# Where a fused attention and MLP block issues its first gate and up weights, and how its first token tiles are transposed

## The chip, the core and the metric

The kernel runs on one core of one Trainium2 chip. The metric is the device time of one execution in microseconds (us), the median of three runs. A core has five engines that run side by side, each taking its own instructions in order: TensorE (PE, matmuls, with its weight loads as PEld), VectorE (DVE), ScalarE (ACT), GpSimd (POOL) and SyncE (SP), which here issues nearly all transfers. TensorE writes its results to PSUM; VectorE and ScalarE carry them on to SBUF, the working memory.

## The reference

One block with a norm ahead of each half: linear attention with 32 heads, then a gated MLP, on 2048 tokens of width 1024. Shortened:

```python
def attention(x, wqkv, wo):                      # x is the normalised input
    q, k, v = split(x @ wqkv)                    # 32 heads of 32
    phi = lambda t: where(t > 0, t + 1, exp(t)) + 1e-6
    pq, pk = phi(q), phi(k)
    kv, z = pk.T @ v, sum(pk)                    # per head, over all tokens
    return (pq @ kv / (pq @ z + 1e-6)) @ wo

def mlp(x, W_gate, W_up, W_down):                # F = 3584
    return (relu(x @ W_gate) * (x @ W_up)) @ W_down

h  = x + attention(layernorm(x), wqkv, wo)
h2 = h + mlp(layernorm(h), W_gate, W_up, W_down)
```

## The kernel before

The large matmuls are done by a Strassen scheme: seven products in place of eight, for which VectorE forms sums of operand blocks (`t1` to `t4` of weights, `hs` of the normalised tokens), and ScalarE takes snapshots (`m`, `u`) of partial results in PSUM. A scheduler orders the instructions of each engine when the kernel is built; the code gives the dependencies and a rough order.

**The start.** The first tiles of 128 tokens are normalised and then transposed on TensorE (`PE_T` is 4), the later ones by a DMA transpose. Sixteen matmuls on zeros keep TensorE busy meanwhile.

```python
def ln_T(t):
    ...                                          # bn_stats, bn_aggr: VectorE
    nc.scalar.activation(out=lnv, ..., func=ACT.Ln, ...)
    nc.scalar.activation(out=rstd, ..., func=ACT.Exp, scale=-0.5)
    xn = bwork.tile([P, D], BF16, tag="hn", bufs=HB, name="xn")
    if t == atiles[0]:
        for k in range(2):                       # the very first tile: VectorE, in two halves
            ks = slice(k * NW, (k + 1) * NW)
            nc.vector.tensor_scalar(out=xn[:, ks], in0=x_sb[:, ks], ...)
        transpose_in(t, xn)
        return
    nc.vector.scalar_tensor_tensor(out=nmr, ...)
    nc.scalar.activation(out=xn[:], in_=x_sb[:], func=ACT.Identity, bias=nmr, scale=rstd)
    if t not in atiles[:PE_T]:
        nc.sync.dma_start_transpose(out=xT[s][i][:, :, r:r + P], in_=xn[:])
        return
    transpose_in(t, xn)

def transpose_in(t, xn):
    s, i, r = place(t)
    for k in range(2):
        pt = pspool.tile([P, KH, P], BF16, tag="D", bufs=1, name="tp")     # one PSUM bank
        for kc in range(KH):                                              # KH = 4
            nc.tensor.transpose(pt[:, kc, :], xn[:, ...], ident[:])
        (nc.scalar.copy if k else nc.vector.tensor_copy)(
            out=xT[s][i][:, k * KH:(k + 1) * KH, r:r + P], in_=pt[:])
```

`k_plain` then multiplies each of the first four tiles with `wk` (16 matmuls of 512 columns for a tile, 8 for each half of `wk`), and `v_plain` with `wv`. `wk` is loaded in two halves of 1 MB, the x tiles between them.

**The attention stage and the weights of the first gate and up quads.** For each tile of tokens there is a chain of steps, each some steps behind the one before it (`LAG`):

```python
def nd():       # numerator and denominator: TensorE; reciprocal by Ln and Exp: ScalarE;
    ...         # the product o_sb: VectorE (L518)
def oT():       # DMA transpose of o_sb, issued by SyncE (L525)
def x_in():     # load of the residual x, SyncE (L529)
def wo_h():     # attn: TensorE (L541); + x and row sums: VectorE (L543); h to DRAM: SyncE (L546);
    ...         # squares, rstd and hn: ScalarE (L553 to L557); hn has two buffers
def hn_T():     # DMA transpose of hn, SyncE (L560); the sums hs follow on VectorE (L117 to L120)
```

Into this stage come the first weights of gate and up: two groups, each of `wg` and `wu` in two halves of 512 KB, so eight loads.

```python
def hold(dst, src):
    nc.gpsimd.tensor_copy(out=dst, in_=src)      # one element

def load(after=None, w_sb=w_sb, v=v, h=h):
    if after is not None:
        hold(w_sb[0:1, 0, h, 0:1], after)
    (nc.sync if after is None else nc.gpsimd).dma_start(
        out=w_sb[:, :, h, :], in_=v[:, :, h, g * GP * P:(g + 1) * GP * P])
...
for step in range(QSTEPS):
    ...
    attn_step(step)
    if step:
        for _ in range(-(-len(early_loads) // (QSTEPS - step))):
            early_loads.pop(0)(held[step][0:1, 0:1])       # held[step] is o_sb of this step
```

The copy of one element of `o_sb` into the weight tile makes the load wait until that step's `o_sb` is written; it paces the loads. The load itself is issued by GpSimd. The later groups, with no pacing, are issued by SyncE.

Of the kernel before, what the change touches and what calls it, by code (L numbers as in the profile page):

```python
# [7 lines left out]
ACT = mybir.ActivationFunctionType  # L8
ALU = mybir.AluOpType
FP32 = mybir.dt.float32  # L10
BF16 = mybir.dt.bfloat16
# [20 lines left out]
def block_kernel(ctx: ExitStack, tc: tile.TileContext, x, wqkv, wo, wg, wu, wd, out, H: int):  # L32
    nc = tc.nc
    P = 128
    xf = x.flatten_outer_dims()
    of = out.flatten_outer_dims()
    S, D = xf.shape
# [6 lines left out]
    NW = 512  # L44
# [3 lines left out]
    KH = KC // 2  # L48
# [23 lines left out]
    GP = 2  # L72
# [67 lines left out]
    def hold(dst, src):  # L140

        nc.gpsimd.tensor_copy(out=dst, in_=src)
# [68 lines left out]
    pspool = psctx.enter_context(tc.tile_pool(name="ps", bufs=1, space=PSUM))  # L211
    with ExitStack() as actx:
# [11 lines left out]
        def load_x(t):  # L224
            x_sb = bwork.tile([P, D], BF16, tag=("x_res", "oT")[atiles.index(t) % 2], bufs=XB, name="x_sb")
            nc.sync.dma_start(out=x_sb[:], in_=xf[t * P:(t + 1) * P, :])
            x_tiles[t] = x_sb
# [4 lines left out]
        def place(t):  # L232
            i, r = divmod(t * P, HS)
            s, r = divmod(r, SW)
            return s, i, r
# [3 lines left out]
        atiles = [t for u in units for t in u]  # L239
# [9 lines left out]
        def ln_T(t):  # L249
            if t not in x_tiles:  # L250
                load_x(t)
            x_sb = x_tiles.pop(t)
            s, i, r = place(t)
            stats = asmall.tile([P, 2, nc.vector.BN_STATS_DIM], FP32, tag="stats", name="stats")
            for k in range(2):
                nc.vector.bn_stats(out=stats[:, k, :], in_=x_sb[:, k * NW:(k + 1) * NW])
            mv = asmall.tile([P, nc.vector.BN_AGGR_DIM], FP32, tag="mv", name="mv")
            nc.vector.bn_aggr(out=mv[:], in_=stats[:])
            sm = asmall.tile([P, 3], FP32, tag="sma", name="sma")
            lnv, rstd, nmr = (sm[:, k:k + 1] for k in range(3))  # L260
            nc.scalar.activation(out=lnv, in_=mv[:, 1:2], func=ACT.Ln, bias=LN_EPS, scale=1.0)
            nc.scalar.activation(out=rstd, in_=lnv, func=ACT.Exp, scale=-0.5)
# [4 lines that stand above are left out]
                    nc.vector.tensor_scalar(out=xn[:, ks], in0=x_sb[:, ks], scalar1=mv[:, 0:1], scalar2=rstd,  # L267
                                            op0=ALU.subtract, op1=ALU.mult)
                transpose_in(t, xn)
                return  # L270
            nc.vector.scalar_tensor_tensor(out=nmr, in0=mv[:, 0:1], scalar=-1.0, in1=rstd, op0=ALU.mult, op1=ALU.mult)
            nc.scalar.activation(out=xn[:], in_=x_sb[:], func=ACT.Identity, bias=nmr, scale=rstd)
            if t not in atiles[:PE_T]:
                nc.sync.dma_start_transpose(out=xT[s][i][:, :, r:r + P], in_=xn[:])
                return
            transpose_in(t, xn)

        def transpose_in(t, xn):
            s, i, r = place(t)
            for k in range(2):  # L280
                pt = pspool.tile([P, KH, P], BF16, tag="D", bufs=1, name="tp")
                for kc in range(KH):
                    nc.tensor.transpose(pt[:, kc, :], xn[:, (k * KH + kc) * P:(k * KH + kc + 1) * P], ident[:])
                (nc.scalar.copy if k else nc.vector.tensor_copy)(
                    out=xT[s][i][:, k * KH:(k + 1) * KH, r:r + P], in_=pt[:])

        rk, k_sums = right_ops(wk_sb, tk)
# [91 lines left out]
        with tc.high_priority():  # L379
            zero = asmall.tile([P, NW], BF16, tag="zero", bufs=1, name="zero")  # L380
            nc.vector.memset(zero[:], 0.0)
            spin = pspool.tile([P, NW], FP32, tag="A", bufs=2, name="spin")
            for n in range(SPIN):
                nc.tensor.matmul(spin[:], lhsT=zero[:, 0:P], rhs=zero[:], start=True, stop=True)
            ln_T(atiles[0])
        ln_T(atiles[1])
        todo = atiles[2:8]
        for t in units[0]:
            k_plain(t)
            ln_T(todo.pop(0))  # L390
# [86 lines left out]
    def load_group(g):  # L477

        tiles, loads = [], []
        for nm, v in (("wg", wg_v), ("wu", wu_v)):  # L480
            w_sb = wpools[g % 2].tile([P, KC, 2, GP * P], BF16, tag=nm, name=nm)
            for h in range(2):
                def load(after=None, w_sb=w_sb, v=v, h=h):
                    if after is not None:
                        hold(w_sb[0:1, 0, h, 0:1], after)
                    (nc.sync if after is None else nc.gpsimd).dma_start(out=w_sb[:, :, h, :], in_=v[:, :, h, g * GP * P:(g + 1) * GP * P])
                loads.append(load)
            tiles.append(w_sb)
        return tiles, loads
# [389 lines left out]
    prv, k = None, 0  # L879
    for r, (wt, f, fi, toks) in enumerate(runs):  # L880
        w = [ops() for _, ops in now]
        later = []
        for n, s in enumerate(toks):
            first = n == 0 and isinstance(wt, int) and fi == 0
# [50 lines left out]
            if k == nwin - 3:  # L935
                for x in range(2):
                    t = wpools[1].tile([P, KC * 2 * GP * P], BF16, tag=("wg", "wu")[x], name="wd")
# [16 lines left out]
    for n in range(2):  # L954
        t = fpool.tile([P, 4 * D], BF16, tag="wraw", bufs=2, name="xd")
# [242 lines left out]
    for n in range(1, len(OUTER)):  # L1198
# [73 lines left out]
        else:  # L1272
            pss = []
            for p in range(4):
# [15 lines left out]
                v = ps[:].rearrange("p (t d) -> p t d", t=2)  # L1290
# [53 lines left out]
```

## Time and profile before

| | |
|---|---|
| median of three runs | 754.87 us (754.65 to 755.37) |
| profiled execution, first to last instruction | 753.1 us |
| mean granted clock of TensorE | 0.989 of full |
| busy share: PE, DVE, ACT, POOL | 97%, 75%, 43%, 2% |
| moved by DMA | 132.04 MB, mean 175 GB/s |

The rows of instructions and waits in the profile name the line, the engine, the operation and what it wrote and read; times without a unit are microseconds from the start of the span, and a bracket at the end of a row gives how long the engine stood idle before it and what ended that. A busy TensorE is not one at full speed: the granted clock tells how fast it went. "SPq" is SyncE issuing a transfer; the time to landing is that from the issue until all data have arrived.

### The profile page before, as it was taken

What the parts mean: (1) busy time and instruction counts of PE and PEld (TensorE: products, weight loads), DVE (VectorE), ACT (ScalarE), POOL (GpSimd) and SP (SyncE); (2) the same over time, 40 slices, a digit from 0 to 9 for tenths busy, and PEclk for the clock granted to TensorE, in tenths of its full rate; (3) what the DMA queues carried; (4) which work ended last, traced back from release to release, by engine and by line L of the source; (5) the groups of instructions that cost most, each with busy time, mean ns of one, the idle gap of its engine ahead of it and who ended that gap; (6) DMA issues with size and microseconds to landing.
All of it is one profiled execution on the core that took longest, in us unless ns stands there. A gap on an engine that the chain in (4) does not pass through costs nothing.

```text
span 753.1 us, 10572 instructions
## 1 busy us (share of the span) xinstructions
PE 729.8 (97%) x3967; PEld 384.2 (51%) x4020; DVE 563.0 (75%) x991; ACT 322.0 (43%) x580; POOL 12.9 (2%) x52
## 2 busy tenths in 40 slices
PE   8999999998988999999999999999999999999997
PEld 3444555444443444444444444444444458888666
DVE  6997654774767677687787778877877559997797
ACT  4785653877567555344444344444434220000000
POOL 0000000021100000000000000000000000000000
PEclk9999999999898999999999999999999999999999
DMA  9765003089587445244936439466574299887922
GB/s 317 165 133 154 0 1 112 1 175 217 111 181 178 125 106 168 70 129 130 260 125 183 140 129 314 149 208 233 196 242 163 85 380 362 312 291 294 315 73 84
DMA packets 139412, 132.04 MB, mean 175 GB/s; under 512 B 50912, under 2 KB 119904, under 8 KB 139360
## 3 DMA queue, kind: packets, MB, share of 16 engines
q1 hardware_dynamic: 127072, 119.03, 52.1%
q10 hardware_dynamic: 11136, 8.13, 3.4%
q0 software_dynamic: 1152, 4.19, 2.3%
q8 instruction: 31, 0.51, 0.3%
q14 instruction: 21, 0.17, 0.1%
HBM read 79.95 MB, written 39.85 MB: 159 GB/s over the span
## 4 chain that ended last, share of the span: by engine, by line
PE 79%; DVE 8%; ACT 6%; DMA 5%; issue 2%; SPq 0%; DVEq 0%; ACTq 0%
PE accA L785 22%; PE accY L785 8%; PE accX L785 8%; PE accA L1117 8%; PE Aq L298 4%; PE attn L541 3%; PE accA L946 3%; PE accX L1117 3%; PE Aq L438 3%; PE accY L1117 2%; DMA hn<-hn 2%; PE Eq L298 2%; PE Aq L705 2%; PE accY L946 2%; PE accX L946 2%
## 5 line engine op out<-in xcount | busy, mean ns | idle before, releaser
L795 ACT ACTIVATE gu<-gu 128x512 bf16<-128x512 bf16 x72 | 45.4, 630 | 131.4 <-DVE gu L794 131.4
L790 ACT COPY snap<-accA 128x1024 f32<-128x1024 f32 x72 | 72.5, 1008 | 36.4 <-PE accA L785 36.2
L541 PE MATMUL attn<-wo_mem,oT 128*128 128x512 bf16 x249 | 61.6, 396 | 1.0 <-DVE o_sb L518 0.4
L785 PEld LDWEIGHTS <-tu 128*128 128x128 f16 x384 | 37.6, 98 | 45.3
L785 PEld LDWEIGHTS <-tg 128*128 128x128 f16 x384 | 37.6, 98 | 45.3
L794 DVE TENSOR_TENSOR gu<-accY,snap 128x1024 bf16<-128x1024 f32 x36 | 43.9, 1218 | 9.7 <-ACT snap L790 9.6
L154 ACT COPY u<-Aq 128x512 f32<-128x512 f32 x56 | 32.4, 582 | 39.9 <-PE Aq L298 19.6
L785 PE MATMUL accA<-hn,tu 128*128 128x512 f16 (+1 forms) x192 | 49.3, 379 | 0.0
L785 PE MATMUL accA<-hn,tg 128*128 128x512 f16 (+1 forms) x192 | 49.3, 379 | 0.0
L794 DVE TENSOR_TENSOR gu<-accX,snap 128x1024 bf16<-128x1024 f32 x36 | 43.9, 1218 | 6.5 <-PE accX L785 3.7
L1117 PEld LDWEIGHTS <-x 128*128 128x128 f16 (+1 forms) x448 | 43.8, 98 | 5.5
L785 PEld LDWEIGHTS <-wu 128*128 128x128 bf16 x288 | 28.2, 98 | 34.0
L785 PEld LDWEIGHTS <-wg 128*128 128x128 bf16 x288 | 28.2, 98 | 34.0
L541 PEld LDWEIGHTS <-oT 128*128 128x128 bf16 x256 | 25.7, 102 | 33.3 <-issue 7.1
L543 DVE SCALAR_TENSOR_TENSOR x_res<-attn,x_res 128x512 bf16<-128x512 f32 x32 | 21.8, 687 | 14.2 <-PE attn L541 14.2
L798 DVE TENSOR_TENSOR hq<-gu 128x512 bf16<-128x512 bf16 x48 | 20.3, 423 | 14.6 <-ACT gu L795 14.5
L298 PEld LDWEIGHTS <-xT 128*128 128x128 bf16 (+1 forms) x192 | 18.6, 98 | 24.2 <-issue 2.7
L1117 PEld LDWEIGHTS <-xs 128*128 128x128 f16 x280 | 27.4, 98 | 3.2
L946 PEld LDWEIGHTS <-x 128*128 128x128 bf16 (+1 forms) x168 | 16.4, 98 | 19.6
L1123 DVE TENSOR_TENSOR snap<-accA,u 128x1024 f32<-128x1024 f32 x16 | 19.5, 1219 | 8.3 <-PE accA L1117 8.1
L518 DVE TENSOR_TENSOR o_sb<-nd,rd 128x384 bf16<-128x384 f32 (+1 forms) x48 | 22.5, 505 | 3.9 <-ACT rd L517 3.8
L785 PE MATMUL accA<-hn,wu 128*128 128x512 bf16 x96 | 24.6, 379 | 0.0
(234 smaller groups left out, 1413.6 us busy)
## 6 DMA issues: line engine op xcount, KB each, us to landing
x<-x_dram SPq DMA_DIRECT2D x17, 896.0 KB, 8.3
x_dram<-hq SPq DMA_DIRECT2D x28, 512.0 KB, 3.0
wraw<-in_B_W_down_dram SPq DMA_DIRECT2D x14, 512.0 KB, 4.9
x_dram<-hq SPq DMA_DIRECT2D x28, 256.0 KB, 2.7
t_dram<-wt SPq DMA_DIRECT2D x28, 256.0 KB, 2.2
xd<-x_dram SPq DMA_DIRECT2D x6, 896.0 KB, 7.4
wg<-in_B_W_gate_dram SPq DMA_DIRECT2D x10, 512.0 KB, 5.3
wu<-in_B_W_up_dram SPq DMA_DIRECT2D x10, 512.0 KB, 7.5
```

The source lines that it names most:

```text
L154: nc.scalar.copy(out=snaps[nm, v], in_=A[v][:])
L298: nc.tensor.matmul(ps[:], lhsT=left[m - 1][:, kc, r + v * P:r + (v + 1) * P], rhs=right[m - 1][:, kc, :], start=(start and kc == 0), stop= ...
L438: nc.tensor.matmul(ps[:], lhsT=rq[m - 1][:, kc, (c + v) * P:(c + v + 1) * P], rhs=left[m - 1][:, kc, :], start=(start and kc == 0), stop=( ...
L518: nc.vector.tensor_tensor(out=ov[:, c0:c0 + n], in0=ndv[:, :, 0:P].rearrange("p k (h e) -> p k h e", h=HPC), in1=rd[:, 0:n, :].unsqueeze(3 ...
L541: nc.tensor.matmul(ps[:], lhsT=st["oT"][:, c, :], rhs=wo_sb[:, c, j * NW:(j + 1) * NW], start=(c == 0), stop=(c == KC - 1))
L543: nc.vector.scalar_tensor_tensor(out=h_sb[:, j * NW:(j + 1) * NW], in0=ps[:], scalar=1.0, in1=h_sb[:, j * NW:(j + 1) * NW], op0=ALU.mult, ...
L785: nc.tensor.matmul(ps[:, v, :], lhsT=w[v][n - 1][:, kc, :], rhs=left[n - 1][:, kc, :], start=(t is not None and kc == 0), stop=(kc == KH - ...
L790: nc.scalar.copy(out=st[nm][:], in_=halves(st["A"]))
L794: add(out=g[:], in0=halves(st[nm]), in1=st[base][:], op=ALU.add)
L795: nc.scalar.activation(out=g[:, 0, :], in_=g[:, 0, :], func=ACT.Relu)
L946: nc.tensor.matmul(ps[:, t * NW:(t + 1) * NW], lhsT=x_tile(n, s, kh)[:, f, (t0 + t) * P:(t0 + t + 1) * P], rhs=w_tile(n, kh)[:, f, :], sta ...
L1117: nc.tensor.matmul(pv[:, tt, :], lhsT=left(m)[:, f, tt * P:(tt + 1) * P], rhs=right(m)[:, f, :], start=(t is not None and f == 0 and tt % ...
```

## The change

Three edits. In the transposes of the very first token tile, the second half goes to a PSUM buffer of another tag, so that the two halves do not share a bank, and both halves are copied out by ScalarE. The second token tile is normalised by ScalarE in two halves, so that its transposes can begin after the first half. And the first gate and up weights are issued by SyncE, as all the later ones are, in place of GpSimd; the pacing copy stays on GpSimd. The aim is an earlier start of TensorE and another way of queueing the weights.

```diff
-            nc.scalar.activation(out=xn[:], in_=x_sb[:], func=ACT.Identity, bias=nmr, scale=rstd)
+            for ks in [slice(k * NW, (k + 1) * NW) for k in range(2)] if t == atiles[1] else [slice(0, D)]:
+                nc.scalar.activation(out=xn[:, ks], in_=x_sb[:, ks], func=ACT.Identity, bias=nmr, scale=rstd)
...
             for k in range(2):
-                pt = pspool.tile([P, KH, P], BF16, tag="D", bufs=1, name="tp")
+                first = t == atiles[0]
+                pt = pspool.tile([P, KH, P], BF16, tag="DE"[k and first], bufs=1 + (k and first), name="tp")
                 for kc in range(KH):
                     nc.tensor.transpose(pt[:, kc, :], xn[:, (k * KH + kc) * P:(k * KH + kc + 1) * P], ident[:])
-                (nc.scalar.copy if k else nc.vector.tensor_copy)(
+                (nc.scalar.copy if k or first else nc.vector.tensor_copy)(
                     out=xT[s][i][:, k * KH:(k + 1) * KH, r:r + P], in_=pt[:])
...
                     if after is not None:
                         hold(w_sb[0:1, 0, h, 0:1], after)
-                    (nc.sync if after is None else nc.gpsimd).dma_start(out=w_sb[:, :, h, :], in_=v[:, :, h, g * GP * P:(g + 1) * GP * P])
+                    nc.sync.dma_start(out=w_sb[:, :, h, :], in_=v[:, :, h, g * GP * P:(g + 1) * GP * P])
```

Building the changed kernel also shows that the scheduler orders some of its other instructions anew. TensorE's program has the same instructions in nearly the same order. SyncE's program has the eight loads among the transposes: the first two after the first transpose of `o_sb`, the others one at a time. VectorE's and ScalarE's programs differ in order over the first 60 us or so, and VectorE's again in the attention stage, where some of the products `o_sb` move ahead of the sums `hs`.

## The prediction

> **What bounds the kernel now.** I read the page's busy times first, then TensorE's waits, then a table of busy time and clock in stretches of 2 us, and last the timelines of the engines around each hole.
>
> ```profile
> PE 729.8 (97%) x3967; PEld 384.2 (51%) x4020; DVE 563.0 (75%) x991; ACT 322.0 (43%) x580; POOL 12.9 (2%) x52
> ...
> PE nd L511 <- DVE o_sb L518: 4.7, 2, 2.8
> PE Aq L438 <- ACT u L154: 3.2, 2, 2.6
> PE tp L283 <- DVE xT L284: 1.4, 1, 1.4
> ```
>
> TensorE sets the time: 753.1 - 729.8 = 23.3 us idle. The wait list is short, and from 315 us to the end it is empty; the change touches only what comes before. So a gain has to come from the first 12 us and from the attention stage at 150 to 240 us. There the table of stretches (columns: stretch, length, busy us of PE, PEld, DVE, ACT, POOL, granted clock, DMA share, GB/s) shows three holes. This is the first:
>
> ```profile
> 184.00:186.00 2.00, 1.35 (x7) 0.57 (x6) 0.00 (x0) 1.94 (x7) 0.00 (x0) 1.00 1.04 271
> 186.00:188.00 2.00, 0.26 (x2) 0.00 (x0) 1.04 (x2) 2.00 (x3) 0.00 (x0) 0.91 0.29 106
> 188.00:190.00 2.00, 0.92 (x2) 0.40 (x3) 1.24 (x4) 1.76 (x9) 0.00 (x0) 0.50 0.46 125
> 190.00:192.00 2.00, 2.00 (x6) 0.73 (x5) 1.39 (x3) 1.24 (x2) 1.06 (x2) 0.50 0.72 145
> 192.00:194.00 2.00, 2.00 (x7) 0.66 (x5) 0.00 (x0) 0.57 (x1) 0.00 (x0) 0.50 0.84 171
> ```
>
> PE idles 0.65 + 1.74 + 1.08 = 3.5 us, and then is busy at half clock: six or seven matmuls in 2 us, where full stretches hold ten or eleven. The lost half is 0.5 x (0.92 + 2 + 2) plus 0.12 x 2 in the next stretch (clock 0.88), 2.7 us. So the hole costs 3.5 + 2.7 = 6.2 us, and its busy half hides in the 97%. By the same sum the hole at 208 to 212 us costs 2.9 idle + 1.5 slow = 4.4 us, and the one at 226 to 232 us 3.4 + 2.8 = 6.2 us. Together 16.8 us.
>
> What opened them, from the timelines of POOL, SP, ACT and DVE:
>
> ```profile
> 175.99 0.88 POOL L486 DMA_DIRECT2D wg<-in_B_W_gate_dram  x1 [0.30 <-POOL wg L142]
> ...
> 176.21 1.46 SPq L560 DMA_TRANSPOSE hn<-hn  x1
> ...
> 183.48 1.15 ACT L553 ACTIVATE hn<-x_res,sm 128x1024 bf16<-128x1024 bf16 x1 [3.06 <-DMA hn<-hn]
> ...
> 210.28 0.42 DVE L117 TENSOR_TENSOR hs<-hn 128x512 f16<-128x512 bf16 x1 [2.75 <-DMA hn<-hn]
> ...
> 225.84 0.42 DVE L117 TENSOR_TENSOR hs<-hn 128x512 f16<-128x512 bf16 x1 [2.92 <-DMA hn<-hn]
> ```
>
> Hole 1: GpSimd issues a 512 KB weight load 0.22 us before SyncE issues the transpose of hn. That transpose takes 7.2 us to land (median of its line 3.5). ScalarE, whose next instruction overwrites the hn buffer, waits 3.06 us, and the snapshots u that TensorE needs stand behind it. Holes 2 and 3: VectorE stands at the first of the operand sums (L117) until a transpose of hn lands, and the normalising multiplies o_sb (L518), which free the PSUM buffers of nd, stand behind it.
>
> **What the Trainium skill says.** "DMA: Bandwidth & Descriptors", section "Queues, rings and completion order": each of the 16 DMA engines goes round between the queue rows that have work, packet by packet, and takes descriptors of one ring in ring order. The trace agrees with the first half: the transpose issued beside the weight load needs 7.2 us, one issued with little beside it (152.91 us) 3.1. For the second half no run here gives a clean case yet. "TensorE: Matmul & The Clock Gate", section "Part 1: The HAM clock gate (the "warmup" mystery)": an idle window of about 3.4 us halves the clock, and a like time of work restores it. The trace agrees: 0.50 after the holes, gone some 6 us later. "PSUM — Partial Sum Buffer", section "Rules for kernel authors", advises that a matmul written while PSUM is read should go to a different bank; that is what the second tag does. The trace shows the opposite now: the second group of transposes waits 1.41 us for VectorE's copy of the first.
>
> **Part 1, the first tile.** The timeline of the start:
>
> ```profile
> 7.38 0.39 PE L283 MATMUL tp<-ident,xn 128*128 128x128 bf16 x4
> ...
> 8.76 0.37 DVE L284 COPY xT<-tp 128x512 bf16<-128x512 bf16 x1
> ...
> 9.18 0.38 PE L283 MATMUL tp<-ident,xn 128*128 128x128 bf16 x4 [1.41 <-DVE xT L284]
> ...
> 10.69 0.56 ACT L284 COPY xT<-tp 128x512 bf16<-128x512 bf16 x1
> ...
> 11.30 0.38 PE L283 MATMUL tp<-ident,xn 128*128 128x128 bf16 x4 [0.18 <-ACT xT L284]
> ```
>
> The first copy waits behind VectorE's statistics of the second tile, the second behind ScalarE's 1.24 us normalisation of that tile. Changed: eight transposes back to back, results at about 7.8 and 8.0; ScalarE is free until 8.88 and copies twice at 0.57 us, 7.8 to 8.95. The first projection matmul can then start at about 8.45 instead of 9.40. Eight of them (8 x 0.216 = 1.7 us) end at 10.2. The second tile's normalisation starts at 9.54 as before; its first half (estimate 0.65 us, from the 0.63 us of other 128x512 activations) is ready at 10.2, so transposes at about 10.25 instead of 11.30: TensorE is 1.0 us ahead. But the second half of wk lands only at 10.3 (issued at 2.29, 8.0 to land), VectorE's first sum waits for it and runs to 11.6 in any case, and from 9.4 to 26 us VectorE is busy 15.57 of 16.60, from 26 to 36 9.81 of 10. It gets rid of one copy of 0.37 us, and that in a place where it would wait. I let half of the 1.0 us survive: 0.5 us.
>
> **Part 2, the weight loads.** Eight issues of 0.88 us leave GpSimd, which is 2% busy: worth nothing in themselves. SyncE gets eight issues of about 0.44 us, and each must wait there in order for GpSimd's one-element copy, which in turn waits for a finished o_sb. What counts is the new place in SyncE's order, which the built program shows. The two loads of the second wg follow differently: one stays ahead of the transpose of 176.21, the other, which collided with it, now stands behind it. So the transpose should land after 3.5 to 4.5 us, near 180.2. ScalarE was idle from 180.4, so its chain moves up by the 3.06 us, the snapshot that came 3 us late is ready within 0.3 to 0.7 us of need, and no half clock follows. Of the 6.2 us I count 5.5.
>
> Hole 2: the collision was wu (203.79), hn (204.10), oT (205.46; 6.3 us to land). The new order is wu, x_res, oT, hn: oT loses hn ahead of it and should land 1.5 to 2 us earlier. And VectorE's order changes: three of the multiplies o_sb and one sum x_res that stood behind L117 now stand ahead of it. I count half: 2.2 us. Hole 3: only one o_sb moves ahead of L117: 2 us of 6.2.
>
> Against it: in the ring a transpose behind a weight load waits for all of it. The first two loads of wg stand between the first and the second oT; 1 MB at the 236 GB/s moved between 160 and 180 us is 4.4 us (estimate), so that oT lands near 162, and TensorE wants it at 163.9. The oT after the second of these weights, SyncE's longer occupation, and work that arrives 6 us earlier at the same DMA queue will open other waits: I take off 3 us.
>
> Sum: 0.5 + 5.5 + 2.2 + 2 - 3 = 7.2 us; 754.9 - 7.2 is about **747.5 us**.
>
> **Rivals.** (a) *The ring is worse than the round.* In order, SyncE is held by each wait for o_sb and every later transpose with it; weights go ahead of urgent oT. For it: DMA shares of 1.0 to 1.2 over 160 to 176 us, and one issue of oT already took 4.58 us. Against it: the copies that the loads wait for come right after the o_sb that the neighbouring transposes need anyhow, so most of these waits are shared. One new hole of 3 to 4 us with its half clock costs 6 us: 752 to 758. (b) *The holes only move.* The bytes are the same, the loop o_sb, oT, attn, hn with its two and three buffers is the bound, and hole 1's gain is given back in hole 2. For it: hole 3 has no weight load beside it. Then only the start and some 2 us remain: 752. (c) *All three holes close*, as the new order of VectorE allows: 754.9 - 0.5 - 16.8 + 1 = 738.5.
>
> **Range and chances.** Between (c) and (a): 740 to 756. Over 2% faster means below 739.8, which needs nearly all of the 16.8 us: 0.07. Over 2% slower means above 770, two or three new holes: 0.015. The rest, 0.915, within 2%.
>
> **What would show it.** Right: the first projection matmul near 8.5 us; the 180 us transpose of hn landing in 3.5 to 4.5 us with no wait of ScalarE of 3 us before L553; no stretch of clock 0.50 at 188 to 194; PE idle near 15 us in all. The start is wrong if VectorE's chain reaches 36 us no sooner than now. The main step is wrong if a clock of 0.50 still follows 180 us, above all with a transpose that took over 6 us behind a weight load in its own queue.

## The result, and the profile after

The changed kernel takes **745.03 us** (median of four runs, 743.46 to 745.54) where the kernel before, run beside it, takes 755.0 (754.65 to 755.37): a ratio of 0.986, 95% interval 0.985 to 0.988. That is 10 us less; the predicted 747.5 stood for 7.4.

How much less it is depends on the executions of the kernel before that stand beside it: when the changed kernel was measured again (e8, below), the difference of the medians was 8.0 us, because the kernel before took 753.58 there. Its time goes with the clock that TensorE was granted. Beside the experiments, the seven of its executions with a mean clock of 1.000 took 747.0 to 747.8 us, and the one with the lowest, 0.985, took 757.3. The two executions of the changed kernel with a clock of 1.000 took 743.2 and 743.5. So some 4 us of the gain are there at full clock, and the rest is the clock: it was 0.994 or more in all eight executions of the changed kernel, and less than that in 70 of 101 of the kernel before.

The page of the changed kernel, busy times, and TensorE's list of waits (columns: what it waited for, us in total, times, longest). Two lines were added ahead of most of the code, so L511 of before is L513 here, L438 is L440, L553 is L555 and L560 is L562:

```profile
PE 721.7 (97%) x3967; PEld 381.7 (51%) x4020; DVE 563.0 (76%) x990; ACT 322.4 (43%) x582; POOL 6.1 (1%) x44
```

```profile
PE Aq L300 <- ACT m L154: 1.8, 2, 1.1
PE tp L285 <- ACT xn L273: 1.6, 2, 1.5
PE nd L513 <- DVE o_sb L520: 1.6, 3, 1.0
PE Aq L440 <- ACT u L154: 1.4, 1, 1.4
PE Eq L707 <- DVE hs L117: 1.3, 1, 1.3
```

The span fell from 753.1 to 741.5 us, by 11.6 us. The same 3967 recorded matmuls are busy for 8.1 us less, and TensorE's idle time, 741.5 - 721.7 = 19.8 us, is only 3.5 less. So most of the gain does not look like a removed wait at all: it is half clock that no longer follows the waits. (Of the 8.1 us, 1.2 are the matmuls on zeros at the very start, 5.12 us here and 6.35 before. That part is no gain: it varies from 5.12 to 6.57 us over the profiled executions, what these matmuls take less counts as idle time instead, and nothing behind them comes earlier, as shown below.) The two long waits for o_sb and u are down from 4.7 to 1.6 and from 3.2 to 1.4; the first two lines come from the first 70 us, not from the attention stage.

The first hole in stretches of 2 us, as before (columns: stretch, length, busy us of PE, PEld, DVE, ACT, POOL, granted clock, DMA share, GB/s):

```profile
184.00:186.00 2.00, 1.80 (x10) 0.69 (x8) 0.75 (x2) 2.00 (x3) 0.00 (x0) 1.00 1.15 316
186.00:188.00 2.00, 0.79 (x3) 0.38 (x4) 1.24 (x3) 2.00 (x9) 0.00 (x0) 1.00 0.40 66
188.00:190.00 2.00, 2.00 (x11) 0.93 (x10) 1.68 (x4) 1.03 (x3) 0.18 (x1) 1.00 0.87 222
190.00:192.00 2.00, 2.00 (x11) 0.94 (x10) 1.59 (x4) 0.86 (x1) 0.00 (x0) 1.00 0.87 229
```

What is left of 6.2 us is 0.20 + 1.21 = 1.4 us of idle time, and the clock stays whole here. SyncE's timeline, and the rows of ScalarE and VectorE that stood in the holes:

```profile
176.54 1.42 SPq L562 DMA_TRANSPOSE hn<-hn  x1
178.05 0.53 SPq L488 DMA_DIRECT2D wg<-in_B_W_gate_dram  x1
178.68 2.81 SPq L527 DMA_TRANSPOSE oT<-o_sb  x1
```

```profile
181.77 1.15 ACT L555 ACTIVATE hn<-x_res,sm 128x1024 bf16<-128x1024 bf16 x1 [1.00 <-DMA hn<-hn]
```

```profile
205.82 0.43 DVE L117 TENSOR_TENSOR hs<-hn 128x512 f16<-128x512 bf16 x1 [0.27 <-DMA hn<-hn]
...
211.32 0.43 DVE L117 TENSOR_TENSOR hs<-hn 128x512 f16<-128x512 bf16 x1 [0.36 <-DMA hn<-hn]
...
217.39 0.43 DVE L117 TENSOR_TENSOR hs<-hn 128x512 f16<-128x512 bf16 x1 [1.58 <-DMA hn<-hn]
```

The weight load that was issued 0.22 us ahead of the transpose of hn, on GpSimd, now stands 1.5 us behind it, on SyncE. The transpose lands after 5.2 us (7.2 before), ScalarE waits 1.00 us for it (3.06 before), and VectorE's waits of 2.75 and 2.92 us for later transposes have shrunk to 0.27, 0.36 and 1.58.

The two waits of VectorE are not alike. The 2.75 us were a second collision of the same kind: in the kernel before, GpSimd issued the eighth load (the second half of the second group's `wu`) at 203.79 and SyncE a transpose of hn at 204.10, which took 6.2 us to land. Now that load is issued by SyncE at 199.06, 2.8 us ahead of the transpose of 201.84, which takes 4.0 us. The 2.92 us had no load beside them: that transpose of hn took 5.4 us before (issued at 220.40), and its counterpart takes 5.5 now (211.88).

The whole attention stage from 180 to 240 us, before and then after, in stretches of 10 us:

```profile
180.00:190.00 10.00, 6.53 (x34) 3.01 (x33) 3.11 (x7) 6.64 (x17) 0.00 (x0) 0.88 0.86 188
190.00:200.00 10.00, 10.00 (x43) 4.32 (x42) 5.96 (x15) 4.82 (x8) 1.06 (x2) 0.78 0.68 134
200.00:210.00 10.00, 8.36 (x44) 3.88 (x43) 7.53 (x21) 5.17 (x17) 1.19 (x2) 1.00 0.57 116
210.00:220.00 10.00, 8.51 (x43) 4.16 (x44) 7.91 (x24) 7.72 (x25) 0.00 (x0) 0.83 0.70 180
220.00:230.00 10.00, 7.00 (x41) 3.54 (x41) 6.99 (x22) 7.07 (x22) 0.00 (x0) 0.93 0.97 180
230.00:240.00 10.00, 9.56 (x33) 3.78 (x33) 7.10 (x20) 6.03 (x15) 0.00 (x0) 0.73 0.83 188
```

```profile
180.00:190.00 10.00, 8.59 (x46) 4.11 (x46) 4.81 (x11) 7.78 (x19) 0.18 (x1) 1.00 0.96 217
190.00:200.00 10.00, 9.80 (x51) 4.63 (x51) 9.04 (x22) 8.07 (x18) 0.31 (x1) 1.00 0.58 105
200.00:210.00 10.00, 9.66 (x61) 5.01 (x61) 9.51 (x30) 6.96 (x26) 0.00 (x0) 1.00 0.97 248
210.00:220.00 10.00, 8.30 (x47) 4.07 (x47) 7.69 (x24) 7.63 (x23) 0.00 (x0) 1.00 1.14 226
220.00:230.00 10.00, 8.78 (x47) 4.25 (x47) 8.57 (x25) 8.48 (x22) 0.00 (x0) 1.00 0.90 212
230.00:240.00 10.00, 9.71 (x51) 4.52 (x51) 8.37 (x21) 5.66 (x17) 0.00 (x0) 1.00 0.54 145
```

Read each row for two losses: the time that PE is not busy, and its busy time multiplied by what the clock lacks of 1.00. The stretch 190 to 200 us of before shows why both are needed: PE is busy for all of 10.00 us, but at 0.78, and does 43 matmuls where the changed kernel does 51 in 9.80. Summed over the six rows, before loses 10.0 idle + 7.5 slow = **17.5 us**, after 5.2 + 0 = **5.2 us**. The difference, 12.3 us, is the whole of the 11.6 us by which the span fell, and a little more. This profile is of the fastest of the four executions of the changed kernel; in e8 below, the same kernel loses 2.9 us to half clock after all.

The start gives nothing. TensorE's timeline of the changed kernel:

```profile
6.14 0.67 PE L285 MATMUL tp<-ident,xn 128*128 128x128 bf16 x8
...
7.21 1.90 PE L333 MATMUL kp<-pq_mem,xT 128*128 128x512 bf16 x8 [0.40 <-ACT xT L286]
10.57 0.40 PE L285 MATMUL tp<-ident,xn 128*128 128x128 bf16 x4 [1.47 <-ACT xn L273]
...
25.68 13.98 PE L351 MATMUL vp<-wv_sb,xT 128*128 128x512 bf16 x63
```

The first projection starts at 7.21 us in place of 9.40, and then TensorE waits 1.47 us for the second tile. The value projections (vp) start at 25.68; in the kernel before they started at 25.62. The first nd of the attention stage comes at 146.87 us, before at 146.51.

### The profile page after: what moved, and what is told of

The parts are those of the page before. It is cut to its first block, busy times and chain, and to the rows that moved or that the text cites. A ratio compares the mean times of both kernels' runs of the same rounds, so it can differ in the third digit from the quotient of the medians.

```text
span 741.5 us, 10570 instructions
## 1 busy us (share of the span) xinstructions
PE 721.7 (97%) x3967; PEld 381.7 (51%) x4020; DVE 563.0 (76%) x990; ACT 322.4 (43%) x582; POOL 6.1 (1%) x44
## 4 chain that ended last, share of the span: by engine, by line
PE 77%; DVE 8%; DMA 7%; ACT 6%; issue 1%; SPq 0%; POOL 0%; DVEq 0%; ACTq 0%
PE accA L787 22%; PE accX L787 8%; PE accY L787 8%; PE accA L1119 8%; PE Aq L300 3%; PE accA L948 3%; PE accX L1119 3%; DMA hn<-hn 3%; PE Aq L440 3%; PE accY L1119 2%; DMA xT<-xn 2%; PE attn L543 2%; PE Aq L707 2%; PE Eq L300 2%; PE accY L948 2%; PE accX L948 2%
## 5 line engine op out<-in xcount | busy, mean ns | idle before, releaser
L543 PE MATMUL attn<-wo_mem,oT 128*128 128x512 bf16 x249 | 57.9, 379 | 1.2 <-DVE o_sb L520 0.4
L787 PE MATMUL accA<-hs,tu 128*128 128x512 f16 x96 | 24.6, 379 | 0.0
```

What stands on the lines that cost most here:

```text
L543: nc.tensor.matmul(ps[:], lhsT=st["oT"][:, c, :], rhs=wo_sb[:, c, j * NW:(j + 1) * NW], start=(c == 0), stop=(c == KC - 1))
L787: nc.tensor.matmul(ps[:, v, :], lhsT=w[v][n - 1][:, kc, :], rhs=left[n - 1][:, kc, :], start=(t is not None and kc == 0), stop=(kc == KH - ...
```

## The experiments

The theory: a weight load on GpSimd, next to a DMA transpose on SyncE, delays the transpose; that delay opens the holes, and two of the eight loads matter, the sixth (second group, `wg`, second half, hole 1) and the eighth (second group, `wu`, second half, hole 2). Rivals: the new order of VectorE is what closes holes 2 and 3; the holes only move; or the start brings the gain. "Loss" below is always the sum just explained, for 180 to 240 us of the profiled execution. A caution for the ratios: the kernel before, run beside the experiments, scatters from 747.0 to 757.3 us, with medians of 749.73, 753.58, 753.12 and 751.78 in the four sets (e1 to e4; e5 to e8; e9 to e11; e12), so the times themselves are compared too. The letters in the expectations name the theories that each of them sets against another.

### Either part alone

e1 is the kernel before with the edit of the loads only:

```diff
-  (nc.sync if after is None else nc.gpsimd).dma_start(out=w_sb[...], ...)
+  nc.sync.dma_start(out=w_sb[...], ...)
```

> The kernel before with the weight loads on SyncE alone, no edit of the start. Theory A (all of the gain comes from the attention stage, the start edits are worth nothing because VectorE's chain reaches 25 us no sooner): 744 to 746, as with the whole change. Theory B (the earlier start is worth 1 us or more): 746.5 to 748.

Measured: 744.79 us (744.31 to 744.93), ratio 0.995 (0.993 to 0.996), loss 6.6 us. It is as fast as the changed kernel.

e2 is the changed kernel with that line put back, so the start edits only:

```diff
-  nc.sync.dma_start(out=w_sb[...], ...)
+  (nc.sync if after is None else nc.gpsimd).dma_start(out=w_sb[...], ...)
```

> The changed start with the weight loads still on GpSimd. Theory A: 754 to 756, the first value projection at 25.6 us as before, the three holes with their half clock all there. Theory B: 753 to 754. If VectorE's order in the first 60 us mattered for the attention stage, the holes would be different ones and the time could leave 752 to 757.

Measured: 754.59 us (751.35 to 756.16), ratio 1.008 (1.005 to 1.010), loss 12.4 us; the load at 176.56 us on GpSimd and ScalarE's wait of 2.93 us are back. All of the gain is the loads'; the start edits are worth nothing, or a little less. (The kernel before took 749.73 beside it, so e2 is 4.9 us slower there. Its four executions had a clock of 0.989 to 0.995, those of the kernel before 0.988 to 1.000; how much of the 4.9 us the edits cost is not shown.)

### Which of the eight loads

e3 is the kernel before with the sixth load alone on SyncE. The orders of TensorE, VectorE and ScalarE stay exactly as before.

```diff
-  (nc.sync if after is None else nc.gpsimd).dma_start(...)
+  (nc.sync if after is None or (g, nm, h) == (1, 'wg', 1) else nc.gpsimd).dma_start(...)
```

> The kernel before with only the sixth of the eight weight loads (the one issued at 175.99) on SyncE; the orders of TensorE, VectorE and ScalarE stay exactly as before. Theory A1 (that one collision with the transpose of hn opens hole 1): hn lands in under 5.5 us, the clock stays full at 188 to 196, 748 to 750.5; holes 2 and 3 stay. Rival (SyncE's ring delays another transpose as much, or the gain is lost in hole 2): 753 to 756.

Measured: 748.94 us (744.28 to 751.65, 12 runs), ratio 0.997 (0.994 to 1.000), not clearly below the kernel before beside it. ScalarE's row in hole 1, and three of the stretches:

```profile
180.53 1.15 ACT L553 ACTIVATE hn<-x_res,sm 128x1024 bf16<-128x1024 bf16 x1 [0.25 <-DMA hn<-hn]
```

```profile
180.00:190.00 10.00, 9.34 (x49) 4.41 (x49) 5.23 (x12) 8.34 (x19) 1.06 (x2) 1.00 0.97 215
...
200.00:210.00 10.00, 6.76 (x37) 3.26 (x36) 6.54 (x21) 5.53 (x18) 0.00 (x0) 0.84 0.82 190
...
220.00:230.00 10.00, 7.30 (x31) 3.10 (x30) 8.42 (x24) 8.19 (x20) 0.00 (x0) 0.83 0.90 214
```

Hole 1 is gone (9.34 busy at full clock; the transpose of hn lands after 4.0 us), by this one load and with no new order of a compute engine. But the stretches 200 to 210 and 220 to 230 still lose 3.24 and 2.70 us to idling and over 1 us each to the clock: VectorE waits there 2.89 and 2.31 us at L117, the first time for the transpose that meets the eighth load (198.09 and 198.35; it lands after 6.3 us). Loss 9.7 us.

e4 is the opposite, the changed kernel with the sixth load alone on GpSimd:

```diff
-  nc.sync.dma_start(...)
+  (nc.gpsimd if after is not None and (g, nm, h) == (1, 'wg', 1) else nc.sync).dma_start(...)
```

> The changed kernel with only the sixth weight load back on GpSimd; the orders of the compute engines as in the changed kernel. Theory A1: hole 1 is back with its half clock, holes 2 and 3 stay mended by VectorE's order: 749 to 752. Rival (what mends is the whole set of loads in one ring, one load more or less does not matter): 744.5 to 746.

Measured: 751.76 us (750.26 to 753.72), ratio 1.003 (1.000 to 1.005), loss 15.2 us. GpSimd's row and ScalarE's:

```profile
176.66 1.01 POOL L488 DMA_DIRECT2D wg<-in_B_W_gate_dram  x1 [0.30 <-POOL wg L142]
```

```profile
188.10 1.15 ACT L555 ACTIVATE hn<-x_res,sm 128x1024 bf16<-128x1024 bf16 x1 [7.02 <-DMA hn<-hn]
```

The transpose of hn was issued at 176.84, 0.18 us after that load, and needs 11.2 us to land. One load on GpSimd takes 6.7 of the 10 us away again.

e5 has the first seven loads on SyncE and the eighth on GpSimd, with the compute engines in the order of before; e6 has only the eighth on SyncE, which brings VectorE's new order with it; e7 has the sixth and the eighth there and leaves the other six on GpSimd:

```diff
-  (nc.sync if after is None else nc.gpsimd).dma_start(...)
+  (nc.sync if after is None or (g, nm, h) in ON_SYNC else nc.gpsimd).dma_start(...)
   # e5: ON_SYNC = all but (1, 'wu', 1);  e6: only (1, 'wu', 1);  e7: (1, 'wg', 1) and (1, 'wu', 1)
```

> The kernel before with loads one to seven on SyncE and only the eighth left on GpSimd. TensorE's, VectorE's and ScalarE's orders are exactly those of before; so this has the queueing of the change without the new order of VectorE. Theory C (hole 1 is mended by the queue, holes 2 and 3 by VectorE's order): hole 1 gone, L117 still holds VectorE for some 3 us twice, the time 748 to 751 on this chip, no better than with the sixth alone. Rival (the queue alone mends all): 744 to 746.

Measured: 754.23 us (752.81 to 755.96, 20 runs), ratio 1.002 (1.000 to 1.003), loss 17.8 us. GpSimd's only load and VectorE's row:

```profile
198.11 1.01 POOL L486 DMA_DIRECT2D wu<-in_B_W_up_dram  x1 [0.30 <-POOL wu L142]
```

```profile
210.21 0.43 DVE L117 TENSOR_TENSOR hs<-hn 128x512 f16<-128x512 bf16 x1 [8.37 <-DMA hn<-hn]
```

Seven loads moved, and no gain, where 748 to 751 was expected: the eighth meets a transpose of hn issued 0.26 us behind it at 198.37, which lands after 11.8 us. VectorE stands for 8.37 us, and TensorE waits 8.4 us for the o_sb behind it.

> The kernel before with only the eighth load on SyncE: VectorE's and TensorE's orders become those of the change, the other seven loads stay on GpSimd. Theory C: hole 1 as before, holes 2 and 3 small with no half clock after them: 747 to 751. Rival (order worth nothing): as the kernel before beside it.

Measured: 748.52 us (746.8 to 751.96), ratio 0.994 (0.991 to 0.996), loss 11.6 us. Hole 1 stays (5.83 us busy of 10 at clock 0.86; the transpose lands after 8.1 us), and VectorE's waits at L117 shrink to 0.46, 0.58 and 1.57 us.

> The kernel before with the sixth and the eighth load on SyncE and the other six on GpSimd. Theory C: both causes are covered, 744 to 746.5, as with all eight on SyncE. Rival (all loads must share one ring): 748 or more.

Measured: 744.06 us (742.25 to 744.93), ratio 0.987 (0.984 to 0.991), loss 6.8 us. Two loads give all of it. Neither gives it alone: each of them meets a transpose of hn of its own. VectorE's new order comes with the eighth load here, in e6 and in the changed kernel, so these runs do not separate the two.

### The changed kernel once more

> The changed kernel once more, on one chip with the others, because the kernel before took 747.5 to 755.6 beside the last experiments: 744 to 746, and a ratio to the kernel before that depends on how that one falls, between 0.986 and 0.996.

Measured: 745.53 us (743.16 to 746.78), ratio 0.989 (0.984 to 0.993). e1, e7, e8 and the first measurement agree within 1.5 us. The profiled execution is the slowest of e8's four, at 746.78 us, and one stretch of it has half clock:

```profile
220.00:230.00 10.00, 8.65 (x28) 3.31 (x28) 6.99 (x21) 6.11 (x15) 0.00 (x0) 0.66 0.92 195
```

That is 1.35 us idle and 0.34 x 8.65 = 2.9 us slow, after 1.8 us of idle time from 210 to 220: 6.1 us, as much as the third hole cost before. In e1 and e7 the clock of this stretch is 0.83. So the third hole is still there, and whether half clock follows it differs between executions.

### Away from the transposes, with no new order

After e6 two readings were still possible: no load beside the transposes, or VectorE's new order. e9 is the kernel before with all eight loads on SyncE and not paced, so that they are issued between 120 and 159 us, before the holes. The orders of TensorE, VectorE and ScalarE are exactly those of before.

```diff
-            early_loads.pop(0)(held[step][0:1, 0:1])
+            early_loads.pop(0)()
```

> The kernel before with all eight loads on SyncE and without the pacing copies: most of the 4 MB then flows before the attention stage, with VectorE's, TensorE's and ScalarE's orders exactly as before (the old order, L117 ahead of the o_sb). Theory C (VectorE's new order is needed for holes 2 and 3): hole 1 gone, two waits of L117 of 2 to 3 us stay, 747 to 751. Rival D (the collisions of loads and transposes are the whole cause, the order only moves L117 away from the collision): L117 waits under 1.5 us, 740 to 744.5.

Measured: **743.03 us** (741.97 to 743.77), ratio 0.987 (0.982 to 0.991), loss 5.3 us: the fastest version of all, by 2 us over the changed kernel. VectorE's rows:

```profile
202.25 0.42 DVE L117 TENSOR_TENSOR hs<-hn 128x512 f16<-128x512 bf16 x1
...
210.37 0.42 DVE L117 TENSOR_TENSOR hs<-hn 128x512 f16<-128x512 bf16 x1 [0.65 <-DMA hn<-hn]
...
215.73 0.43 DVE L117 TENSOR_TENSOR hs<-hn 128x512 f16<-128x512 bf16 x1 [1.91 <-DMA hn<-hn]
```

The expectation that rested on VectorE's order, 747 to 751, missed. With the old order, no load near, and transposes of hn that land after 4.3 us (issued 176.60) and 3.4 us (198.81), the first sum does not wait at all: holes 1 and 2 are gone, and the new order was not needed for that. The third hole is only smaller:

```profile
210.00:220.00 10.00, 7.38 (x43) 3.56 (x42) 7.72 (x23) 7.70 (x23) 0.00 (x0) 1.00 0.97 202
220.00:230.00 10.00, 9.84 (x43) 4.29 (x43) 7.51 (x21) 6.88 (x18) 0.00 (x0) 0.83 1.02 206
```

These are 2.62 us idle and 0.17 x 9.84 = 1.67 slow, 4.3 us where it was 6.2; the transpose that VectorE waits for (1.91 us) takes 5.0 us with no load near it. e9 changes the queue and the pacing at once. Paced on SyncE (e1) the time is 1.8 us higher; unpaced on GpSimd was not tried.

### The queue or the engine that issues

e11 is the kernel before with the sixth load issued by ScalarE. The profile lists ScalarE's queue as hardware_dynamic, like SyncE's and unlike GpSimd's (software_dynamic), but it is a queue of its own:

```diff
+  (nc.scalar if (g, nm, h) == (1, 'wg', 1) and after is not None else nc.sync if after is None else nc.gpsimd).dma_start(...)
```

> The kernel before with the sixth load issued by ScalarE's queue: a ring of its own as with GpSimd, but without GpSimd's software issue. Theory F (a ring of its own beside SyncE's is what lets the load delay the transpose): the transpose of hn at 176 takes 6.5 to 8 us to land and hole 1 stays; 752 to 756. Rival (GpSimd's way of issuing is what slows it): it lands in 4 to 5.5 us as with SyncE, 747 to 751.

Measured: 750.9 us (746.76 to 754.48, 20 runs), ratio 0.997 (0.995 to 1.000), loss 14.4 us; the time is below the 752 to 756 of theory F, the landing is as it said. The load is issued at 175.47, the transpose of hn at 175.94, and it lands after 6.5 us:

```profile
182.47 1.15 ACT L553 ACTIVATE hn<-x_res,sm 128x1024 bf16<-128x1024 bf16 x1 [2.31 <-DMA hn<-hn]
```

So the load need not be GpSimd's to delay the transpose. Whether the second queue does it, or only the place just ahead, is not separated: no run has a load on SyncE less than 1 us ahead of a transpose of hn. All landings of a transpose of hn beside the sixth or the eighth load:

| the load stands | runs (time of the transpose's issue) | landed after |
|---|---|---|
| on GpSimd, 0.2 to 0.3 us ahead | before (176.21, 204.10), e2 (176.78, 203.47) | 7.2, 6.2, 7.1, 6.0 us |
| | e3 (198.35), e6 (175.98), e11 (201.68) | 6.3, 8.1, 6.3 us |
| | e4 (176.84), e5 (198.37) | 11.2, 11.8 us |
| on ScalarE, 0.5 us ahead | e11 (175.94) | 6.5 us |
| on SyncE, 1.5 to 1.6 us behind | after, e1, e3, e5, e7, e8, e10, e12 | 4.0 to 5.2 us |
| on SyncE, 2.8 us ahead | after, e1, e4, e6, e7, e8, e10, e12 | 3.7 to 4.9 us |
| none near | e9 (176.60, 198.81) | 4.3, 3.4 us |

ScalarE's one case lies inside GpSimd's range. Later in the stage, beside other transposes and with no load near, a transpose of hn took up to 5.7 us (e6, issued at 216.96), so the cases on SyncE show no clear delay. The two longest are the runs in which that load alone was left on GpSimd; why they are the longest is not known.

### The start

Two runs ask why an earlier first projection is worth nothing. The reading was that VectorE, busy for 15.6 of the 16.6 us from 9.4 to 26 us in both kernels, is the bound. e10 is the changed kernel with the four sums of `wk` (L133 to L136) on GpSimd:

```diff
-            nc.vector.tensor_tensor(out=t1, in0=b12, in1=b11, op=ALU.subtract)
+            nc.gpsimd.tensor_tensor(out=t1, in0=b12, in1=b11, op=ALU.subtract)   # and t2, t3, t4
```

> The changed kernel with the four sums of wk on GpSimd, which takes some 4.8 us of work from VectorE between 10 and 31 us. Theory E (the earlier start is lost because VectorE's chain sets when TensorE reaches the value projections): these start at 23.5 to 25 us instead of 25.7, and the time falls by 0.5 to 2 us, to 743 to 745. Rival (the landing of the second half of wk, or ScalarE, sets it): 25.5 us and 744.5 to 746.5. If GpSimd's reads slow VectorE: later than 26 us and slower.

Measured: 754.61 us (750.89 to 755.6, 20 runs), ratio 1.002 (1.001 to 1.004); a miss. The value projections start at 30.75 us. The loss from 180 to 240 us is only 5.8, so all the rest was lost earlier. GpSimd's row and VectorE's beside it:

```profile
10.50 4.06 POOL L133 TENSOR_TENSOR pq_mem<-pq_mem 128x2048 f16<-128x2048 bf16 x1 [7.92 <-DMA pq_mem<-in_A_wqkv_dram]
```

```profile
11.99 2.72 DVE L336 TENSOR_SCALAR e<-e 128x512 bf16<-128x512 bf16 x1
```

VectorE's tensor_scalar takes 2.72 us in place of 0.28, and ends at 14.71, just after GpSimd's sum (10.50 + 4.06 = 14.56). "SBUF — State Buffer", section "SBUF: two separate sides", in the Trainium skill gives a reason: VectorE and GpSimd share a pair of ports, and where an instruction of VectorE in a two-port mode, or with two inputs from SBUF, meets one of GpSimd, the one that starts first holds the pair to its end and the other is blocked. The two ends agree with that; whether this tensor_scalar ran in such a mode the trace does not show. So this run loads VectorE instead of relieving it, and leaves the question open.

e12 therefore takes the work away: the changed kernel without the four sums. The products that need a sum are formed with a plain block of `wk` in its place, so part of the computation is left out.

```diff
         rk, k_sums = right_ops(wk_sb, tk)
+        rk = (b11, b21, b22, b21, b11, b22, b12)      # plain blocks of wk
+        k_sums = lambda: None
```

> The changed kernel with the four sums of blocks of wk left out (part of the computation is missing: the products that need a sum are formed with a plain block in its place). TensorE's instructions stay the same, VectorE has four instructions of 1.2 us fewer in the first 30 us or so. Theory A (VectorE's work, and the first of these sums standing ahead of the copy of the second tile, ate what the start edits won): the copy of the second tile's first half starts near 11.0 us in place of 11.67, and the value projections start between 23.3 and 24.5 us in place of 25.68 (TensorE's own work from 7.21 us would fill the time to about 23.2). Median 742 to 744.5. Rival E (the transfers set the start, the second half of wk and the x tiles): value projections at 25.3 us or later, median 745 to 746.

Measured: 745.84 us (743.61 to 747.93, 15 runs), ratio 0.992 (0.990 to 0.995). TensorE's timeline (its lines stand 3 further down):

```profile
7.90 1.90 PE L336 MATMUL kp<-pq_mem,xT 128*128 128x512 bf16 x8 [0.45 <-ACT xT L286]
...
24.52 5.78 PE L354 MATMUL vp<-wv_sb,xT 128*128 128x512 bf16 x26
```

The value projections start at 24.52, 1.16 us earlier, though the first projection itself started 0.69 us later; the stretch between them shrank from 18.47 to 16.62 us. So VectorE's load did bind there, as the theory had it, though 24.52 is just outside its 23.3 to 24.5. Two things missed: the copy of the second tile starts at 11.62, not 11.0, because the statistics of the third tile, whose x landed at 11.0, now stand ahead of it; and the time is no lower, 745.84 where the theory had 742 to 744.5 and its rival 745 to 746. The first nd comes at 147.9 us, later than in the changed kernel (146.87): TensorE's waits from 38 to 74 us, for v_sb, wo_mem and m (4.4 us together), took the lead back, while VectorE was busy for 29.9 of the 32 us from 26 to 58. What arrives early at the start waits later.

### The sum over all runs

One line for each profiled execution: its span, the loss from 180 to 240 us, and the rest (span minus loss).

| kernel | span | loss | rest |
|---|---|---|---|
| before | 753.1 | 17.5 | 735.6 |
| e5, e6, e7 | 753.6, 746.7, 742.7 | 17.8, 11.6, 6.8 | 735.8, 735.1, 735.9 |
| e1, e3, e9, e11 | 743.1, 745.9, 741.8, 750.8 | 6.6, 9.7, 5.3, 14.4 | 736.5, 736.2, 736.5, 736.4 |
| after, e2, e4, e8 (with the start edits) | 741.5, 749.5, 751.8, 744.9 | 5.2, 12.4, 15.2, 8.3 | 736.3, 737.1, 736.6, 736.6 |
| e10, e12 (start edits and other sums) | 752.7, 744.9 | 5.8, 7.0 | 746.9, 737.9 |

Over the twelve executions with the sums of `wk` as they were, the span moves by 12 us and the rest stays between 735.1 and 737.1. The loss in these 60 us explains the span. The four with the start edits have a mean rest of 736.65, the eight without 736.0: the start edits cost some 0.6 us, if anything.

## Why the prediction was right, point by point

**The sum** was 0.5 + 5.5 + 2.2 + 2 - 3 = 7.2 us, which from 754.9 gives 747.7 (the prediction wrote 747.5); measured 745.03, a gain of 10.0. The mechanism held: two loads beside two transposes. Its terms did not all.

**Start, +0.5: wrong, it is about -0.6.** The working for the first tile was exact where it could be: from the first transpose to the first projection 8.45 - 7.38 = 1.07 us were predicted, and 7.21 - 6.14 = 1.07 measured. The whole came 1.24 us earlier because the matmuls on zeros ended earlier. What failed was "I let half of the 1.0 us survive". For the second tile the transposes came at 10.57, but VectorE's copy of their result at 11.67, before at 11.73: the first sum of `wk` stood ahead of it, the very wait that the prediction named. Even the 1.2 us that e12 freed further on did not reach the attention stage. By the prediction's own test (VectorE's chain no sooner at 36 us) the start was to be called wrong, and it is: VectorE begins its sums at L117 at 36.13 us, before at 36.17.

**Hole 1, 5.5 of 6.2: 4.8 came.** Right: no clock of 0.50 at 188 to 194 us, and no wait of 3 us ahead of L553. Off in size: the transpose took 5.2 us, not 3.5 to 4.5, ScalarE waits 1.00 us and TensorE 1.35 for the snapshot, 1.4 us in all. The collision as the cause is shown three ways: put back alone (e4), taken away alone (e3), and moved in time (e9).

**Holes 2 and 3, 2.2 + 2: undercounted, in hole 2.** Outside hole 1 the loss fell from 17.5 - 6.2 = 11.3 to 5.2 - 1.4 = 3.8 us, so 7.5 us came where 4.2 were counted, and that with the new waits of this stage already inside. The prediction saw the collision of hole 2, but credited only the oT behind it and VectorE's new order. The wait that opened the hole was for the transpose of hn itself, 6.2 us in landing, and it went from 2.75 to 0.27 us when that landed in 4.0. e9 closes hole 2 with the old order. For hole 3, 2 us of 6.2 was fair: "Hole 3 has no weight load beside it" is true, and what is left at 210 to 230 us is 4.3 us in e9, 6.1 in e8 and 2.9 in the first profile of the changed kernel, which had no half clock there. Why it shrinks at all was not separated.

**New waits, -3: hardly any in this profile.** They are part of the 3.8 us just named; the longest single waits left in the stage are 1.35 and 1.28 us, and no half clock followed them. In e8 it did, for 2.9 us. The long issue that was feared did occur (2.81 us for oT at 178.68, which lands after 5.6), and the clock stayed at 1.00 from 180 to 220 us.

In all, 4.8 + 7.5 = 12.3, less 0.6 for the start, is 11.7 against the 11.6 us of the two spans. The medians differ by less, 10.0, because single executions scatter. The errors cancelled in part, which is luck: the start and hole 1 were counted 1.8 us too high, the other terms 6.3 too low.

**PE idle near 15 us: wrong, 19.8.** The idle time that left the attention stage (10.0 - 5.2 = 4.8) does not show in full: from 0 to 40 us TensorE is busy 35.66 us where it was 36.88. That difference is the 1.2 us by which the matmuls on zeros were shorter in this execution, so it is no new wait. Without it some 18.6 us would stand, still well above 15.

**Rivals.** (a), the ring is worse: refuted by e1. (b), the holes only move: wrong for the whole change, but what e3 shows in part, and e5 in full. (c), all three close at no cost: two of them do, the third in part; its 16.8 us were 12.3 in the first profile and 17.5 - 8.3 = 9.2 in e8.

**Left open.** "Issuing engines are not separate DMA queues" in "DMA: Bandwidth & Descriptors" of the Trainium skill says that transfers of all engines interleave on the same 16 DMA engines, and that several issuers save only the time of issue. Here a load just ahead on another engine went with a landing of a transposing transfer that was 1.7 to 7.5 us later than the 4.3 with none near (table above). The round between queues that the prediction cited would give the direction, but no run tests it. The same 512 KB load is 144 packets in GpSimd's queue (e4) and adds 1040 packets to ScalarE's (e11); what that does to a transpose beside it, and why GpSimd's cases reach from 6.0 to 11.8 us, is not settled.

## What to carry to other kernels

Where one short transfer is waited for and a bulk load is not, keep the load out of a second queue beside it: put it in the same queue behind it, or issue it well before. Two of eight loads made the whole difference here, so look for the load issued a fraction of a microsecond ahead of the transfer that lands late, and move that. Count a hole in TensorE's work with the half clock after it, and expect no gain from an earlier start while another engine is full behind it.

## What was not expected of the hardware

- A 512 KB load on GpSimd, issued 0.2 to 0.3 us ahead, went with a landing time of 6.0 to 11.8 us for a transpose of 256 KB (nine cases); with that load on SyncE, behind or 2.8 us ahead, it was 3.7 to 5.2.
- GpSimd's sum of 128x2048 elements takes 4.06 us, VectorE's 1.2, and a VectorE instruction of 0.28 us beside it took 2.72: moving work to an idle engine slowed the full one.
- The kernel before scatters over 10 us between executions (747.0 to 757.3), along with its mean granted clock (1.000 to 0.985). The changed kernel (twice measured), e1, e7 and e9, whose sixth and eighth loads are not on GpSimd, stay between 742.0 and 746.8.
